# Five matmuls in place of six for units 2 and 14 of batches 1 to 7, with their sum and difference on VectorE

## The chip, the cores and the metric

The kernel runs on one core of a Trainium2 chip. The metric is the device time of one execution in microseconds (us). The engines are called by the profile's names: PE is TensorE, DVE is VectorE, ACT is ScalarE, POOL is GpSimd, SP is SyncE, which here issues DMAs. "L444" is line 444 of the kernel before.

## What is computed

The input x has 8 batches of 3072 rows with 256 columns. Each batch goes through a Fourier transform along both axes, of which the real part is kept; then each row goes through a layer with three weight matrices, an elementwise maximum of the three products, and an output matrix:

```python
X = np.fft.fft(np.fft.fft(x, axis=1), axis=2).real      # 8 x 3072 x 256
X = X.reshape(24576, 256)
h = np.maximum(np.maximum(X @ w1, X @ w2), X @ w3)      # 24576 x 768
out = h @ w_out                                         # 24576 x 256
```

## The kernel before, in words

The transform along the rows of a batch ends in two tables for half of its rows, an even part tE and an odd part tO (128 x 1536 in bf16); a row and its mirror row are the sum and the difference of the two. The transform along the columns is folded into the weights: gE, gO and gD hold (w2 - w1) and (w3 - w1) behind it, index 0 for the first difference and 1 for the second, with gD = -2 gO but for a correction of one row. With them the hidden layer is max(0, second product, third product), and what w1 gives is added in the last step.

**Units.** The main loop runs over 8 batches x 18 units. A unit is one of three blocks of 512 row pairs and one of six slices of 128 hidden columns (UNITS = 18, NJC = 6). The unit with number g gives two tiles of 128 x 512, hp for the rows and hm for their mirror rows. `begin(g, ...)` makes hp, `finish(g, ...)` makes hm, usually one unit later.

- A unit that is not split has six matmuls of 512 columns. `unit_plus` puts gE and gO products of both differences into two PSUM banks, pse2 and pse3 (L436, L437). `unit_out` makes hp: ACT writes relu(pse2) as stmp (L450), DVE takes the maximum with pse3 (L451). `unit_minus` then adds the gD products to the same two banks (L444), which turns the sum into the difference, and `unit_out` makes hm from them.
- A split unit (odd numbers from 7 on) has five. `third(g)` runs two units ahead (one ahead for unit 7): two matmuls give the even product e3 (L755) and the odd product d3 (L757) of the second difference in two banks; ACT copies -0.5 x d3 to SBUF as odd3 (L759); DVE adds a term to e3 and writes even3 (L760); POOL makes even3 + odd3 and even3 - odd3, plus3 and minus3 (L764). `begin` has the two matmuls of the first difference alone (L771, L772) and one DVE operation that takes the maximum with 0 and plus3 (L773); `finish` has one gD matmul and the like with minus3 (L785).

**Banks.** PSUM has eight banks here: ps_f with three, used by `third` and by all pieces of the transform and of the output step that need one; ps_l1 with two for pse2; ps_w3 with one for pse3 of even units; ps_o with two for the output step's po and for pse3 of odd units.

**Order.** The schedule is written out by hand: each engine runs its instructions in the order of the program. For each g the loop does this: if the unit before is split, `finish` of it, then `begin(g)`; else `begin(g)` first and then `finish` of the unit before. Then `third` of a coming unit; `scatter`, which issues waiting indirect stores on POOL; ten steps of the output step of an earlier block (`l2_some(10)`: matmuls L460, L475 and L483 into po, then DVE's ot at L488 and the stores on SP); and last what a plan has put at this place, pieces of the next batch's transform above all. The pieces that matter here are s (L369: two matmuls into a bank of ps_f, emptied by ACT at L372) after units 1, 2 and others, and k (L411: some six small matmuls into a bank of ps_f, emptied by ACT at L413) after units 12 to 16. `x0` (L399) waits for a small POOL copy (`u`, L394). Batch 7 has no pieces of a next batch.

Of the kernel before, what the change touches and what calls it, by code (L numbers as in the profile page):

```python
# [9 lines left out]
FP32 = mybir.dt.float32  # L10
BF16 = mybir.dt.bfloat16
INT32 = mybir.dt.int32
AX = mybir.ActivationFunctionType
ALU = mybir.AluOpType
# [36 lines left out]
def kernel(  # L51
# [9 lines left out]
    nc = tc.nc  # L61

    B, S, D = x.shape
# [3 lines left out]
    TOKB = 512  # L67
    NHALF = 1536
    UNITS = 3 * NJC
# [9 lines left out]
    ps_f = ctx.enter_context(tc.tile_pool(name="ps_f", bufs=3, space=bass.MemoryType.PSUM))  # L79
# [94 lines left out]
    for r in (0, 6, 11):  # L174
        n = {0: 6, 6: 5, 11: 4}[r]
# [25 lines left out]
    def scal(out, in0, s1, op0, s2=None, op1=None, eng=None):  # L201
# [8 lines left out]
                                   op0=ALU.mult, op1=ALU.add)  # L210
# [3 lines left out]
                                   op0=ALU.mult, op1=ALU.add)  # L214
# [5 lines left out]
                                   op0=ALU.mult, op1=ALU.add)  # L220
# [7 lines left out]
    half = gen.tile([128, 256], FP32, tag="half")  # L228
# [7 lines left out]
    for fc in range(2):  # L236
        scal(pf[:, fc:fc + 1], pidx, float(128 * fc), ALU.add)
        nc.vector.scalar_tensor_tensor(
            out=vm[:, fc * 256:(fc + 1) * 256].rearrange("p (k c) -> p k c", c=128),
            in0=dvec.unsqueeze(1).to_broadcast([128, 2, 128]), scalar=pf[:, fc:fc + 1],  # L240
            in1=half.rearrange("p (k c) -> p k c", c=128), op0=ALU.mult, op1=ALU.add)
# [12 lines left out]
                          in_=par.unsqueeze(1).to_broadcast([128, 2, 2]))  # L254
# [311 lines left out]
    def scatter():  # L566

        while waiting:
            at_row, lo, ot = waiting.pop(0)
            stored(nc.gpsimd.indirect_dma_start(  # L570
                out, bass.IndirectOffsetOnAxis(
                    ap=rows_m[0:128 - lo, at_row: at_row + 1], axis=0),
                ot[lo:128, 256:512], None), "scattered", ("scattered", "direct"))
            nc.gpsimd.memset(mark, 0.0)

    def l2_some(n):
        while n > 0 and l2_queue:
            try:
                next(l2_queue[0])
                n -= 1  # L580
            except StopIteration:
                l2_queue.pop(0)
# [37 lines left out]
    for (s0, s1) in HALVES:  # L620
        for h in range(2):
            load_x(1, s0, s1, h)
        if s0 == 0:
            nc.gpsimd.dma_start(out=wout_bf.rearrange("p (jc c) -> p jc c", jc=NJC),
                                in_=moe_w_out.rearrange("(jc p) c -> p jc c", jc=NJC))
# [15 lines left out]
    for u in range(3):  # L641
# [7 lines left out]
                       in1=adj.unsqueeze(1).to_broadcast([128, B, 12]), op=ALU.add)  # L649
# [4 lines left out]
    ps_w3 = ctx.enter_context(tc.tile_pool(name="ps_w3", bufs=1, space=bass.MemoryType.PSUM))  # L654
# [3 lines left out]
    s_pool = ctx.enter_context(tc.tile_pool(name="sums", bufs=3))  # L658
# [79 lines left out]

    sums = {}

    def is_split(g):
        return g % 2 == 1 and 7 <= g < B * UNITS

    def operands(g):
        b, u = divmod(g, UNITS)
        blk, jc = divmod(u, NJC)
        mm = mixes[b]
        ts = slice(blk * TOKB, (blk + 1) * TOKB)
        return slice(jc * 128, (jc + 1) * 128), mm.tE[:, ts], mm.tO[:, ts], mm.vb[:, ts], jc

    def third(g):

        js, te, to, vb, jc = operands(g)
        e3 = ps_f.tile([128, TOKB], FP32, name="e3", tag="ps")
        nc.tensor.matmul(e3, gE[1][:, js], te, start=True, stop=True)  # L755
        d3 = ps_f.tile([128, TOKB], FP32, name="d3", tag="ps")
        nc.tensor.matmul(d3, gD[1][:, js], to, start=True, stop=True)  # L757
        even3, odd3 = (s_pool.tile([128, TOKB], FP32, name=n, tag=n) for n in ("even3", "odd3"))
        nc.scalar.activation(out=odd3, in_=d3, func=AX.Copy, scale=-0.5)  # L759
        nc.vector.scalar_tensor_tensor(out=even3, in0=vb, scalar=wcol[:, jc:jc + 1], in1=e3,  # L760
                                       op0=ALU.mult, op1=ALU.add)
        sums[g] = [s_pool.tile([128, TOKB], BF16, name=n, tag=n) for n in ("plus3", "minus3")]
        for dst, op in zip(sums[g], (ALU.add, ALU.subtract)):
            nc.gpsimd.tensor_tensor(out=dst, in0=even3, in1=odd3, op=op)  # L764

    def begin(g, dst):

        js, te, to, _, jc = operands(g)
        if is_split(g):
            pse2 = ps_l1.tile([128, TOKB], FP32, name="pse2", tag="pse2")  # L770
            nc.tensor.matmul(pse2, gE[0][:, js], te, start=True, stop=False)  # L771
            nc.tensor.matmul(pse2, gO[0][:, js], to, start=False, stop=True)  # L772
            nc.vector.scalar_tensor_tensor(out=dst, in0=pse2, scalar=0.0, in1=sums[g][0],  # L773
                                           op0=ALU.max, op1=ALU.max)
            return (pse2,)
        pses = unit_plus(te, to, jc, TOKB, *((ps_o, "po") if g % 2 else (ps_w3, "pse3")))
        unit_out(pses, dst, TOKB)
        return pses

    def finish(g, pses, dst):  # L780

        js, te, to, _, jc = operands(g)
        unit_minus(pses, to, jc)
        if is_split(g):
            nc.vector.scalar_tensor_tensor(out=dst, in0=pses[0], scalar=0.0, in1=sums.pop(g)[1],  # L785
                                           op0=ALU.max, op1=ALU.max)
        else:
            unit_out(pses, dst, TOKB)

    prev = None  # L790
    for g in range(B * UNITS):
        b, u = divmod(g, UNITS)
        blk, jc = divmod(u, NJC)
        mm = mixes[b]
        last = b == B - 1 and blk == 2
        if jc == 0:
            hp = h_pool.tile([128, NJC, TOKB], BF16, name="hp", tag="hp")
            hm = h_pool.tile([128, NJC, TOKB], BF16, name="hm", tag="hm")
            if last:
                flipped = []  # L800
                for t, name in ((mm.tE, "tEr"), (mm.tO, "tOr")):
                    fl = h_pool.tile([128, TOKB], BF16, name=name, tag=name)
                    flipped.append(fl)
                    nc.gpsimd.tensor_copy(fl, t[:, 3 * TOKB - 1: 2 * TOKB - 1: -1])
        if prev is not None and is_split(prev[0]):
            finish(*prev)
            prev = None
        pses = begin(g, hp[:, jc, :])
        if prev is not None:
            finish(*prev)  # L810
        prev = (g, pses, hm[:, jc, ::-1] if last else hm[:, jc, :])
        for lead in (1, 2):
            if is_split(g + lead) and (lead == 1) == (g + lead == 7):
                third(g + lead)
        scatter()
        l2_some(10)
        if b == B - 1 and u in (1, 3):
            if u == 1:
                middle = l2_mid()
            next(middle, None)  # L820
        for fn in plan.get((b, u), ()):
            fn()
        if jc == NJC - 1:
            l2_some(1000)
            if g == B * UNITS - 1:
                finish(*prev)
            l2_queue.append(l2_last(hp, hm, mm.tE, mm.tO, flipped) if last else
                            l2_block(b, blk, hp, hm, mm.tE, mm.tO))
# [32 lines left out]
```

## Time and profile before

| | |
|---|---|
| three runs | 406.56, 406.56, 405.85 us; median 406.56 us |
| the profiled execution | 405.21 us, of which the span of its instructions is 403.4 us |
| granted clock of PE, mean over the span | 0.991 |
| pace | 45.5 us a batch |

The pace is the distance of equal instructions in neighbouring batches: the matmul L755 of unit 3 starts at 169.63 us in batch 3 and at 215.09 us in batch 4. A profile names each engine's busy time, the span in 40 equal slices, whom an engine waited for, and every instruction's start and length. The costliest groups of the units, one line each (line, engine, operation, result and operands with their shapes, count; busy us, mean ns of one; idle us of the engine before them and what ended it):

```profile
L450 ACT ACTIVATE stmp<-pse 128x512 bf16<-128x512 f32 x150 | 89.9, 600 | 62.1 <-PE pse L444 45.2
L764 POOL TENSOR_TENSOR plus<-even,odd 128x512 bf16<-128x512 f32 x69 | 87.9, 1274 | 39.8 <-DVE even L760 32.2
L773 DVE SCALAR_TENSOR_TENSOR hp<-pse,plus 128x512 bf16<-128x512 f32 x69 | 47.6, 690 | 50.6 <-PE pse L772 21.1
L444 PE MATMUL pse<-tO,gD 128*128 128x512 bf16 x218 | 70.8, 379 | 1.0 <-DVE hp L451 0.4
L488 DVE TENSOR_TENSOR ot<-po,even 128x512 f32<-128x512 f32 x92 | 62.9, 683 | 0.0
L451 DVE TENSOR_TENSOR hp<-pse,stmp 128x512 bf16<-128x512 f32 x75 | 51.5, 686 | 10.3 <-ACT stmp L450 8.7
L760 DVE SCALAR_TENSOR_TENSOR even<-vb,wcol,e 128x512 f32<-128x512 bf16 x69 | 51.0, 739 | 0.0
L785 DVE SCALAR_TENSOR_TENSOR hm<-pse,minus 128x512 bf16<-128x512 f32 x69 | 47.2, 684 | 1.8 <-PE pse L444 0.4
L759 ACT ACTIVATE odd<-d 128x512 f32<-128x512 f32 x69 | 41.3, 598 | 6.6
```

The last column is read first: it says for which group its engine stood still. The mean of a matmul is its whole time through the array; matmuls follow each other more closely than that, so PE's pace is read from start to start in the timeline.

### The profile page before, as it was taken

Reading aid. Unit: us, or ns where it says so; the run is one execution under the profiler, and the core shown is the slowest. Engines: PE = TensorE matmul, PEld = TensorE weight load, DVE = VectorE, ACT = ScalarE, POOL = GpSimd, SP = SyncE. Lnnn points to the kernel's source line nnn. Section 1 sums busy time; section 2 is a strip of 40 time slices with the busy share of each in tenths; the row PEclk is TensorE's granted clock in tenths of the full one; section 3 lists DMA queues with packets and bytes.
Section 4 is the critical chain, followed back from the end, with each engine's and each line's share of the span. In section 5 each row is a group of like instructions: output and inputs, shape, how many; then the busy total and the mean of one; then the engine's idle time right before and its main releaser. Section 6 shows DMA issues by size and latency. Waiting matters only on the chain.

```text
span 403.4 us, 8304 instructions
## 1 busy us (share of the span) xinstructions
PE 383.7 (95%) x2695; PEld 236.7 (59%) x2743; DVE 319.6 (79%) x542; ACT 261.2 (65%) x466; POOL 322.1 (80%) x403
## 2 busy tenths in 40 slices
PE   7589899999999999999999999999999999999995
PEld 2245456656665566656665566656665566666574
DVE  7869887877887887877887887877887887887982
ACT  2565879768865778568875778568865546635430
POOL 7376279787988799897988799897988699788991
PEclk9799999999999999999999999999999999999999
DMA  8999968495765958394764958495532653322225
GB/s 122 196 187 174 176 180 158 118 169 131 178 141 121 185 147 166 109 178 116 192 149 109 190 146 160 115 160 143 149 107 78 149 141 100 94 70 67 89 81 142
DMA packets 69692, 56.30 MB, mean 140 GB/s; under 512 B 35040, under 2 KB 65248, under 8 KB 68452
## 3 DMA queue, kind: packets, MB, share of 16 engines
q0 software_dynamic: 23376, 26.27, 34.5%
q1 hardware_dynamic: 45106, 28.86, 27.6%
q10 hardware_dynamic: 1168, 0.65, 0.6%
q8 instruction: 21, 0.34, 0.3%
q14 instruction: 21, 0.17, 0.2%
HBM read 38.15 MB, written 31.71 MB: 173 GB/s over the span
## 4 chain that ended last, share of the span: by engine, by line
PE 73%; DMA 9%; DVE 5%; issue 5%; POOL 4%; ACT 3%; SPq 1%; ACTq 0%; DVEq 0%; POOLq 0%
PE po L460 25%; PE pse L444 10%; PE pse L436 7%; DMA out_dram<-ot 6%; PE pse L437 5%; PE pse L771 4%; PE po L483 4%; PE d L757 3%; PE pse L772 3%; PE e L755 3%; DVE even L760 3%; PE ps L411 2%; DMA xt<-in_x_dram 2%; PE pl L475 2%; POOL minus L764 2%
## 5 line engine op out<-in xcount | busy, mean ns | idle before, releaser
L450 ACT ACTIVATE stmp<-pse 128x512 bf16<-128x512 f32 x150 | 89.9, 600 | 62.1 <-PE pse L444 45.2
L764 POOL TENSOR_TENSOR plus<-even,odd 128x512 bf16<-128x512 f32 x69 | 87.9, 1274 | 39.8 <-DVE even L760 32.2
L570 POOL DMA_INDIRECT out_dram<-ot,rows_m x92 | 102.4, 1113 | 17.9 <-issue 8.3
L773 DVE SCALAR_TENSOR_TENSOR hp<-pse,plus 128x512 bf16<-128x512 f32 x69 | 47.6, 690 | 50.6 <-PE pse L772 21.1
L764 POOL TENSOR_TENSOR minus<-even,odd 128x512 bf16<-128x512 f32 x69 | 87.6, 1269 | 0.0
L460 PE MATMUL po<-wout_bf,hp 128*128 128x256 bf16 x576 | 86.1, 273 | 0.3
L460 PE MATMUL po<-wout_bf,hm 128*128 128x256 bf16 x576 | 78.6, 273 | 0.0
L444 PE MATMUL pse<-tO,gD 128*128 128x512 bf16 x218 | 70.8, 379 | 1.0 <-DVE hp L451 0.4
L460 PEld LDWEIGHTS <-hp 128*128 128x128 bf16 x576 | 56.4, 98 | 26.1
L460 PEld LDWEIGHTS <-hm 128*128 128x128 bf16 x576 | 56.4, 98 | 16.3
L488 DVE TENSOR_TENSOR ot<-po,even 128x512 f32<-128x512 f32 x92 | 62.9, 683 | 0.0
L451 DVE TENSOR_TENSOR hp<-pse,stmp 128x512 bf16<-128x512 f32 x75 | 51.5, 686 | 10.3 <-ACT stmp L450 8.7
L436 PE MATMUL pse<-tE,gE 128*128 128x512 bf16 x147 | 55.6, 378 | 1.6 <-ACT stmp L450 0.2
L451 DVE TENSOR_TENSOR hm<-pse,stmp 128x512 bf16<-128x512 f32 x75 | 51.7, 689 | 5.9 <-ACT stmp L450 2.1
L760 DVE SCALAR_TENSOR_TENSOR even<-vb,wcol,e 128x512 f32<-128x512 bf16 x69 | 51.0, 739 | 0.0
L437 PE MATMUL pse<-tO,gO 128*128 128x512 bf16 x130 | 49.2, 379 | 0.7 <-ACT tO L413 0.4
L785 DVE SCALAR_TENSOR_TENSOR hm<-pse,minus 128x512 bf16<-128x512 f32 x69 | 47.2, 684 | 1.8 <-PE pse L444 0.4
L759 ACT ACTIVATE odd<-d 128x512 f32<-128x512 f32 x69 | 41.3, 598 | 6.6
L129 ACT COPY xt<-xt 64x762 bf16<-64x762 bf16 (+1 forms) x48 | 40.2, 838 | 1.1
L372 ACT CAST tb<-ps 128x512 bf16<-128x512 f32 x46 | 24.8, 589 | 21.7 <-PE ps L369 21.7
L444 PEld LDWEIGHTS <-gD 128*128 128x128 bf16 x219 | 21.2, 97 | 23.2 <-issue 5.0
L483 PE MATMUL po<-gw,tO 128*128 128x512 bf16 x86 | 32.7, 380 | 0.0
(155 smaller groups left out, 462.4 us busy)
## 6 DMA issues: line engine op xcount, KB each, us to landing
yb<-db SPq DMA_DIRECT2D x7, 833.0 KB
xt<-in_x_dram POOLq DMA_DIRECT2D x14, 384.0 KB, 8.3
out_dram<-ot SPq DMA_DIRECT2D x56, 96.0 KB
out_dram<-ot SPq DMA_DIRECT2D x64, 64.0 KB
db<-tb SPq DMA_DIRECT2D x21, 192.0 KB
vb<-vd SPq DMA_DIRECT2D x23, 128.0 KB
xt<-in_x_dram POOLq DMA_DIRECT2D x7, 400.0 KB
xt<-in_x_dram POOLq DMA_DIRECT2D x7, 368.0 KB, 5.6
```

The lines of the kernel that those rows point to most:

```text
L436: nc.tensor.matmul(pse[:, 0:n], gE[i][:, js], te, start=True, stop=False)
L437: nc.tensor.matmul(pse[:, 0:n], gO[i][:, js], to, start=False, stop=True)
L444: nc.tensor.matmul(pse, gD[i][:, js], to, start=False, stop=True, skip_group_check=True)
L450: nc.scalar.activation(out=stmp[:, 0:n], in_=pses[0][:, 0:n], func=AX.Relu)
L451: nc.vector.tensor_tensor(out=dst, in0=src3, in1=stmp[:, 0:n], op=ALU.max)
L460: nc.tensor.matmul(po, hcols(jc), wout_bf[:, jc * 256:(jc + 1) * 256], start=False, stop=(jc == NJC - 1), skip_group_check=True)
L483: nc.tensor.matmul(po, to[:, cp], gw[:, 256:768], start=True, stop=True)
L488: nc.vector.tensor_tensor(out=ot.rearrange("p (h c) -> p h c", h=2), in0=po.rearrange("p (h c) -> p h c", h=2), in1=lin.unsqueeze(1).to_br ...
L570: stored(nc.gpsimd.indirect_dma_start(out, bass.IndirectOffsetOnAxis(ap=rows_m[0:128 - lo, at_row: at_row + 1], axis=0), ot[lo:128, 256:51 ...
L760: nc.vector.scalar_tensor_tensor(out=even3, in0=vb, scalar=wcol[:, jc:jc + 1], in1=e3, op0=ALU.mult, op1=ALU.add)
L764: nc.gpsimd.tensor_tensor(out=dst, in0=even3, in1=odd3, op=op)
L773: nc.vector.scalar_tensor_tensor(out=dst, in0=pse2, scalar=0.0, in1=sums[g][0], op0=ALU.max, op1=ALU.max)
```

## The change

Units 2 and 14 of batches 1 to 7 (14 units), which were not split, are split too, in a form of their own. Their `third` runs one unit ahead, before the `third` of the odd unit behind them. Their e3 goes into the bank of ps_w3 and d3 into one of ps_f. ACT makes no odd3 and POOL no sums: DVE makes plus3 and minus3 straight from d3's bank and even3, with the factors -0.5 and 0.5.

```diff
+    def on_dve(g):
+        return g >= UNITS and g % UNITS in (2, 14) and g < B * UNITS
+
     def is_split(g):
-        return g % 2 == 1 and 7 <= g < B * UNITS
+        return (g % 2 == 1 and 7 <= g < B * UNITS) or on_dve(g)
...
     def third(g):
 
         js, te, to, vb, jc = operands(g)
-        e3 = ps_f.tile([128, TOKB], FP32, name="e3", tag="ps")
+        pool3, tag3 = (ps_w3, "pse3") if on_dve(g) else (ps_f, "ps")
+        e3 = pool3.tile([128, TOKB], FP32, name="e3", tag=tag3)
         nc.tensor.matmul(e3, gE[1][:, js], te, start=True, stop=True)
         d3 = ps_f.tile([128, TOKB], FP32, name="d3", tag="ps")
         nc.tensor.matmul(d3, gD[1][:, js], to, start=True, stop=True)
-        even3, odd3 = (s_pool.tile([128, TOKB], FP32, name=n, tag=n) for n in ("even3", "odd3"))
-        nc.scalar.activation(out=odd3, in_=d3, func=AX.Copy, scale=-0.5)
+        even3 = s_pool.tile([128, TOKB], FP32, name="even3", tag="even3")
+        if not on_dve(g):
+            odd3 = s_pool.tile([128, TOKB], FP32, name="odd3", tag="odd3")
+            nc.scalar.activation(out=odd3, in_=d3, func=AX.Copy, scale=-0.5)
         nc.vector.scalar_tensor_tensor(out=even3, in0=vb, scalar=wcol[:, jc:jc + 1], in1=e3,
                                        op0=ALU.mult, op1=ALU.add)
         sums[g] = [s_pool.tile([128, TOKB], BF16, name=n, tag=n) for n in ("plus3", "minus3")]
+        if on_dve(g):
+            for dst, half in zip(sums[g], (-0.5, 0.5)):
+                nc.vector.scalar_tensor_tensor(out=dst, in0=d3, scalar=half, in1=even3,
+                                               op0=ALU.mult, op1=ALU.add)
+            return
         for dst, op in zip(sums[g], (ALU.add, ALU.subtract)):
             nc.gpsimd.tensor_tensor(out=dst, in0=even3, in1=odd3, op=op)
...
         for lead in (1, 2):
-            if is_split(g + lead) and (lead == 1) == (g + lead == 7):
+            if is_split(g + lead) and (lead == 1) == (g + lead == 7 or on_dve(g + lead)):
                 third(g + lead)
```

The order around unit 2 (unit 14 is alike, with 12, 13, 14 and 15), as the two programs have it:

| loop turn | before | after |
|---|---|---|
| 1 | begin 1, finish 0, third 3, l2, pieces | begin 1, finish 0, **third 2**, third 3, l2, pieces |
| 2 | finish 1, begin 2 (four matmuls), l2, pieces | finish 1, begin 2 (two matmuls), l2, pieces |
| 3 | begin 3, finish 2 (two matmuls), third 5, l2, pieces | finish 2 (one matmul), begin 3, third 5, l2, pieces |

## The prediction

> **What bounds the kernel now.** I read the page from the top (busy shares, the 40 slices), then the waits of TensorE (PE) alone from 60 to 400 us, then the timeline at the places that the change touches, then the groups by shape for the prices. The busy shares and two of the slice rows:
>
> ```profile
> PE 383.7 (95%) x2695; PEld 236.7 (59%) x2743; DVE 319.6 (79%) x542; ACT 261.2 (65%) x466; POOL 322.1 (80%) x403
> ...
> PE   7589899999999999999999999999999999999995
> DVE  7869887877887887877887887877887887887982
> ```
>
> PE is at 9 tenths from the sixth slice to the last but one; no other engine is. The waits of PE from 60 to 400 us, the whole answer:
>
> ```profile
> PE psx L399 <- POOL x0u L394: 1.2, 6, 0.2
> ```
>
> In 340 us PE waited 1.2 us for anybody. So there is no slack on it: a matmul taken from PE shortens the run by its step, and any new wait of PE lengthens the run by its length. The timeline of batch 4 around the place where unit 2's work will stand (columns: start, duration, engine, line, operation, result and operands):
>
> ```profile
> 214.23 0.38 PE L771 MATMUL pse<-tE,gE 128*128 128x512 bf16 x1
> 214.44 0.38 PE L772 MATMUL pse<-tO,gO 128*128 128x512 bf16 x1
> 214.66 0.59 PE L444 MATMUL pse<-tO,gD 128*128 128x512 bf16 x2
> 214.93 0.69 DVE L773 SCALAR_TENSOR_TENSOR hp<-pse,plus 128x512 bf16<-128x512 f32 x1 [0.64 <-PE pse L772]
> 215.08 0.60 ACT L450 ACTIVATE stmp<-pse 128x512 bf16<-128x512 f32 x1 [0.93 <-PE pse L444]
> 215.09 0.38 PE L755 MATMUL e<-tE,gE 128*128 128x512 bf16 x1
> ...
> 215.31 0.38 PE L757 MATMUL d<-tO,gD 128*128 128x512 bf16 x1
> 215.52 0.82 PE L460 MATMUL po<-wout_bf,hm 128*128 128x256 bf16 x6
> 215.71 0.69 DVE L451 TENSOR_TENSOR hm<-pse,stmp 128x512 bf16<-128x512 f32 x1
> ...
> 216.18 0.38 PE L483 MATMUL po<-gw,tO 128*128 128x512 bf16 x1
> ...
> 216.31 0.74 DVE L760 SCALAR_TENSOR_TENSOR even<-vb,wcol,e 128x512 f32<-128x512 bf16 x1
> 216.39 0.38 PE L460 MATMUL po<-wout_bf,hp 128*128 128x256 bf16 x2
> ...
> 216.71 0.62 PE L369 MATMUL ps<-xt,tab 128*64 128x512 bf16 x4
> ```
>
> Matmuls overlap, so I count steps from start to start: 0.215 us for 512 columns (214.23, 214.44, 214.66), 0.11 us for 256 (six from 215.52 to 216.18). VectorE (DVE) starts one 0.69 us operation 0.60 us after the other (215.71, 216.31). It starts 0.11 us after the matmul that it waits for (L772 ends at 214.82, L773 starts at 214.93), and a matmul that waits for DVE starts 0.05 to 0.06 us after it (a hp ending at 38.07 releases the L444 matmul at 38.12). One DVE operation that reads the result of the one before starts 0.03 us behind its end (L22 and L24, 8.69 and 0.43 long, then 9.15).
>
> **The change, part by part.** It touches 14 units, two in each of seven batches.
>
> *Matmuls.* Each unit had six (L436/L437 four, L444 two) and gets five (two new ones for e3 and d3, two for its begin, one for its finish). PE's built list is 28 rows shorter, 14 matmuls and their 14 weight loads. 14 x 0.215 = **-3.0 us**.
>
> *The bank of e3.* This is the step that decides. e3 of unit 2 (14) takes the one bank of ps_w3, and its matmul is issued one unit ahead, directly behind the two L444 matmuls of unit 0 (12). These write that same bank, and its last reader is unit 0's hm operation on DVE (L451), which itself needs ScalarE's L450 of the other bank. In the built program of the changed kernel this matmul waits for that hm operation. Before, the next tenant was unit 2's own begin, a whole unit later, and it found the bank free. In the rows above, the place is where L755 now starts, at 215.09; the hm ends at 215.71 + 0.69 = 216.40, and e3 can start at 216.46. PE stands for 216.46 - 215.09 = 1.37 us; it works in order, so everything behind waits too, the L460 matmuls first. I read the same two rows at all 14 places (where the matmul's record is missing, its weight load's end plus 0.115 us, as at the places that have both). Unit 2: 1.37 us in six batches, 1.54 in batch 2. Unit 14: 1.66 us in batches 1 to 5, where ScalarE first empties a tO bank (L413) and L450 comes 0.3 us later, and 1.37 in batches 6 and 7. Sum: 6 x 1.37 + 1.54 + 5 x 1.66 + 2 x 1.37 = **+20.8 us**.
>
> *The sums on DVE.* The unit loses two L451 operations (0.69) and gets even3 (row L760, 0.74), two sums and two of the begin/finish form (L773 0.69, L785 0.68): +2.1 us a unit, some 30 us in all, so DVE would be busy about 349 us of some 427. The two sums, one PSUM and one fp32 SBUF operand and a bf16 result, have no row: L488 (PSUM and fp32, 0.68) and L760 (0.74) bound them; I take 0.69, by L773, which has its operation and its result type. Most of this lies beside PE, in DVE's 84 us of idle time. Two places are not covered.
>
> First, the bank of d3 is now free only when the second sum has read it, where ScalarE's copy (L759) freed it before; of the pieces that follow in the same unit, the second takes this bank in the built program. Unit 2 of batch 4: e3 at 216.46, even3 216.95 to 217.69, sums 217.72 to 218.41 and 218.32 to 219.01. PE after e3 has three steps more (d3 and unit 3's pair), so the l2 matmuls begin at 217.32, the first s piece at 218.51 (1.19 later, as 215.52 to 216.71 above) and the second at 218.78; it may start at 219.07: 0.29 us. Unit 14 in the same way: e3 at 247.31, second sum done at 249.86, second k piece due at 249.51, free at 249.92: 0.41 us.
>
> Second, unit 14's hp operation stands on DVE behind even3 of unit 15, an ot (L488) and hm of unit 13. That chain ends at 252.31; the finish matmul is due at 252.11 and starts at 252.37: 0.26 us. For unit 2 the same chain ends at 221.45 and the matmul is due at 221.73: nothing.
>
> Batch 7 has no pieces behind it. So 6 x 0.29 + 6 x (0.41 + 0.26) = **+5.7 us**, bounded by nothing (if ScalarE and DVE, which catch up during the wait, take it up) and by twice as much (if another ot falls into each chain).
>
> *Work that goes elsewhere.* ScalarE loses two L450 a unit (14 x 1.2 = 17 us) and GpSimd gets nothing; neither is what PE waits for, so I cost it at nothing. The cover is PE's own queue; were it gone, the most to gain would be the 1.2 us of psx waits. GpSimd's sums for units 3 and 15 come some 2.6 us later, behind two more operations of DVE, while PE is 1.7 us later; their readers have a unit's length in hand. Transfers keep their order, so I cost them at nothing as well.
>
> *Sum.* -3.0 + 20.8 + 5.7 = **+23.5 us**. The profiled execution took 405.2 us (span 403.4 and 1.8 around it), which gives 428.7; the runs' median is 1.4 us above it, and on 406.56 the sum gives 430.1. I predict 430.
>
> **The clock.** A wait of this length may also cost granted clock. The windows of the trace show half clock once:
>
> ```profile
> 10.00:12.00 2.00, 0.52 (x3) 0.13 (x2) 1.68 (x4) 0.23 (x1) 1.99 (x4) 1.00 1.26 201
> 12.00:14.00 2.00, 0.84 (x6) 0.25 (x5) 1.36 (x6) 1.13 (x3) 1.63 (x5) 1.00 1.31 195
> 14.00:16.00 2.00, 1.01 (x5) 0.42 (x5) 1.65 (x12) 1.18 (x3) 0.26 (x1) 0.54 1.27 210
> 16.00:18.00 2.00, 0.91 (x3) 0.38 (x4) 1.90 (x5) 1.21 (x3) 0.00 (x0) 0.50 1.14 247
> ...
> 22.00:24.00 2.00, 1.28 (x11) 0.66 (x9) 1.20 (x2) 1.97 (x5) 1.96 (x3) 1.00 0.73 225
> 24.00:26.00 2.00, 1.32 (x11) 0.68 (x12) 0.01 (x1) 1.04 (x4) 2.00 (x4) 1.00 1.21 179
> ```
>
> The second column is the window's length, then PE's busy time; the clock is the third from the end. It fell after 4 us in which PE worked 1.36 us, and held at 1.00 where it worked 2.60 of 4 (22 to 26 us). A single new wait leaves PE more than half of any 4 us, so I keep the full clock. The Trainium skill (TensorE: Matmul & The Clock Gate, section "A second HAM failure mode: psum-queue depth-cycling") speaks against me: at bf16 and 512 columns, short idles between groups that cycle through PSUM banks made the clock swing between half and full. That page of the skill (section "What's actually happening") puts the fall after an idle window of about 3.4 us, which the trace's 4 us agree with and a wait of 1.7 us would not reach.
>
> **Rivals.**
> - *Faster: the bank is free in time.* If hm of unit 0 (12) were done less than 0.215 us after e3 is due, the saved matmul would win: with no wait -3.0 us, 403.5. The place is the bank of ps_w3, the price 0.215 us a unit. All 14 places show 1.37 us or more, and what sets it, L450 then L451, is unchanged. 4%.
> - *Slower still: DVE falls behind.* Around the changed units DVE has 4.9 us of work in one unit, where PE needs 2.6. If its queue is not worked off before the next unit's banks are wanted, each of the 12 units with pieces loses one more DVE step of 0.6 us: +7.2, 437. Against it: the unit after has only two or three DVE operations. 12%.
> - *The clock halves behind each wait.* The half-clock stretch above cost 0.46 x 2 + 0.50 x 4 + 0.24 x 2 = 3.4 us (the 20 to 22 window has 0.76); 14 of them are +48, 478. 3%.
> - *The change does not do what it says.* The built list has the matmuls gone and the sums on DVE: under 1%.
>
> **How the numbers follow.** Forecast 80%, the others as above. The low end leaves out the 5.7 us of second waits (424.4) and lets PE win back some 3 us of them elsewhere: 421. The high end is the DVE rival with 1 us: 438. Faster than before by over 0.2% (0.8 us, about what a measurement of this kernel can tell from no change) 4%, within it 1%, slower 95%.
>
> **What would show it.** Right: the e3 matmul of the 14 units with an idle time before it, put down to DVE hm L451, of 1.2 to 1.5 us each (the idle column counts from the end of the matmul before, 0.16 us later than its step); shorter ones at the second s or k piece, put down to the second sum; PE's share falling to about 90%; the clock at 1.00. Wrong: no idle time before these matmuls; idle time before others in larger sum; DVE at 9 tenths throughout; a clock under 1.00 in the later slices.

## The result, and the profile after

| | before | after |
|---|---|---|
| median of six runs, us | 406.04 (405.48 to 406.56) | 431.0 (430.25 to 431.74) |
| ratio | | 1.061 (95% interval 1.060 to 1.063) |
| span of the profiled execution, us | 403.4 | 429.5 |
| distance of two batches, us | 45.5 | 48.9 |

The kernel became 6% slower, 25 us, where 23.5 were forecast. The profiled execution is the slowest of the six runs, so its span stands 26.1 us above that of before, and sums are made against the median here. The busy shares and the slices:

```profile
PE 385.1 (90%) x2681; PEld 236.4 (55%) x2729; DVE 346.6 (81%) x584; ACT 247.5 (58%) x438; POOL 322.1 (75%) x403
...
PE   6588899899898998899898998899798998899885
...
DVE  6969788877888888887887888887788888887892
```

PE has 14 matmuls less and yet a longer span; its nines are broken by an eight (once a seven) every two or three slices. VectorE gained 27 us of work and stands at 7 or 8 tenths nearly everywhere; its nines are the second, the fourth and the last slice but one. The waits of PE from 60 us to the end, the whole answer (us in total, times, longest):

```profile
PE e L759 <- DVE hm L451: 18.8, 14, 2.1
PE pse L444 <- DVE hp L784: 1.9, 2, 1.2
PE ps L411 <- DVE minus L771: 1.6, 6, 0.3
PE ps L369 <- DVE minus L771: 1.0, 6, 0.2
```

Where before there was one row of 1.2 us there are four, and all of them name VectorE. 14 waits are at the new e3 matmul, one for each changed unit. The timeline at unit 2 of batch 4, the place that the prediction worked through:

```profile
225.95 0.59 PE L444 MATMUL pse<-tO,gD 128*128 128x512 bf16 x2
...
226.37 0.60 ACT L450 ACTIVATE stmp<-pse 128x512 bf16<-128x512 f32 x1 [0.93 <-PE pse L444]
...
227.00 0.69 DVE L451 TENSOR_TENSOR hm<-pse,stmp 128x512 bf16<-128x512 f32 x1
...
227.74 0.38 PE L759 MATMUL e<-tE,gE 128*128 128x512 bf16 x1 [1.19 <-DVE hm L451]
...
229.00 0.69 DVE L771 SCALAR_TENSOR_TENSOR plus<-d,even 128x512 bf16<-128x512 f32 x1
...
229.61 0.68 DVE L771 SCALAR_TENSOR_TENSOR minus<-d,even 128x512 bf16<-128x512 f32 x1
...
230.34 0.41 PE L369 MATMUL ps<-xt,tab 128*64 128x512 bf16 x2 [0.16 <-DVE minus L771]
```

The two L444 matmuls start at 225.95, so the next was due 2 x 0.215 us later, at 226.38; it starts at 227.74, 0.05 us after hm ends at 227.69. That is 1.36 us (the idle column shows 1.19, since it counts from the end of the matmul before). The last row is the second s piece, held by the second sum. The granted clock was 1.00 here, and in every window of 50 us from 50 to 400 us (the window's length, busy time of PE, PEld, VectorE, ScalarE and GpSimd, then the clock):

```profile
200.00:250.00 50.00, 46.42 (x327) 28.74 (x331) 40.79 (x64) 32.33 (x57) 40.63 (x49) 1.00 0.67 142
```

### The profile page after: what moved, and what is told of

It is laid out like the page before. It is cut to its first block, busy times and chain, and to the rows that moved or that the text cites. A ratio compares the mean times of both kernels' runs of the same rounds, so it can differ in the third digit from the quotient of the medians.

```text
span 429.5 us, 8247 instructions
## 1 busy us (share of the span) xinstructions
PE 385.1 (90%) x2681; PEld 236.4 (55%) x2729; DVE 346.6 (81%) x584; ACT 247.5 (58%) x438; POOL 322.1 (75%) x403
## 4 chain that ended last, share of the span: by engine, by line
PE 62%; DVE 14%; POOL 8%; issue 6%; ACT 5%; DMA 4%; DVEq 0%; ACTq 0%; POOLq 0%
PE po L460 21%; PE pse L444 8%; PE pse L436 6%; DVE even L766 4%; PE pse L437 4%; PE e L759 4%; PE pse L782 3%; PE po L483 3%; PE pse L783 3%; DVE hm L451 3%; POOL minus L775 3%; PE d L761 2%; DVE minus L771 2%; ACT stmp L450 2%; POOL plus L775 2%
## 5 line engine op out<-in xcount | busy, mean ns | idle before, releaser
L450 ACT ACTIVATE stmp<-pse 128x512 bf16<-128x512 f32 x122 | 72.9, 598 | 57.8 <-PE pse L444 41.6
L784 DVE SCALAR_TENSOR_TENSOR hp<-pse,plus 128x512 bf16<-128x512 f32 x83 | 57.1, 687 | 33.6 <-PE pse L783 18.3
L444 PE MATMUL pse<-tO,gD 128*128 128x512 bf16 x203 | 67.4, 379 | 3.9 <-DVE hp L784 1.9
L460 PEld LDWEIGHTS <-hp 128*128 128x128 bf16 x576 | 56.4, 98 | 26.1
L766 DVE SCALAR_TENSOR_TENSOR even<-vb,wcol,e 128x512 f32<-128x512 bf16 x83 | 61.4, 740 | 6.5 <-PE e L759 6.5
L796 DVE SCALAR_TENSOR_TENSOR hm<-pse,minus 128x512 bf16<-128x512 f32 x83 | 56.9, 686 | 10.8 <-PE pse L444 10.8
L451 DVE TENSOR_TENSOR hp<-pse,stmp 128x512 bf16<-128x512 f32 x61 | 41.9, 687 | 9.4 <-ACT stmp L450 8.7
L759 PE MATMUL e<-tE,gE 128*128 128x512 bf16 x83 | 31.4, 378 | 19.3 <-DVE hm L451 18.8
L451 DVE TENSOR_TENSOR hm<-pse,stmp 128x512 bf16<-128x512 f32 x61 | 42.0, 689 | 5.5 <-ACT stmp L450 2.7
L436 PE MATMUL pse<-tE,gE 128*128 128x512 bf16 x119 | 45.0, 378 | 1.5 <-ACT stmp L450 0.2
L437 PE MATMUL pse<-tO,gO 128*128 128x512 bf16 x103 | 39.0, 379 | 0.7 <-ACT tO L413 0.4
```

The source lines that it names most:

```text
L436: nc.tensor.matmul(pse[:, 0:n], gE[i][:, js], te, start=True, stop=False)
L437: nc.tensor.matmul(pse[:, 0:n], gO[i][:, js], to, start=False, stop=True)
L444: nc.tensor.matmul(pse, gD[i][:, js], to, start=False, stop=True, skip_group_check=True)
L450: nc.scalar.activation(out=stmp[:, 0:n], in_=pses[0][:, 0:n], func=AX.Relu)
L451: nc.vector.tensor_tensor(out=dst, in0=src3, in1=stmp[:, 0:n], op=ALU.max)
L460: nc.tensor.matmul(po, hcols(jc), wout_bf[:, jc * 256:(jc + 1) * 256], start=False, stop=(jc == NJC - 1), skip_group_check=True)
```

## The experiments

Three theories were set against each other. The *queue theory* is the prediction's: PE, which works in order, stands until operations on VectorE have been reached and done, and pays each such wait in full. The *shared-bank theory* says that the single bank of ps_w3 is the cause, and that e3 elsewhere would cost nothing. The *load theory* says that VectorE's extra operations cost the time, wherever they stand. Ratios are to the kernel before, run on the same chip (95% intervals in brackets); times are medians.

**early_bank: the wait without the change.** The kernel before, and in it (cut: the two helpers, and the part of `begin` that then makes the other bank's two matmuls alone):

```diff
+        if early(g + 1):           # units 2 and 14 of batches 1 to 7
+            pse3_early(g + 1)      # the two gE/gO matmuls into ps_w3's bank
         for lead in (1, 2):
             if is_split(g + lead) and (lead == 1) == (g + lead == 7):
                 third(g + lead)
```

> The kernel before, with all its six matmuls and its sums; only the two matmuls of units 2 and 14 (batches 1 to 7) into the bank of ps_w3 are issued one unit ahead, directly behind the finish of unit 0 (12). Queue theory (PE stands until the hm operation of unit 0 or 12 has read the bank): the 14 first waits alone, 406.0 + 20.8 = 427, each 1.2 or 1.5 us of idle time before the early matmul. Load theory (DVE's extra operations cost the time, wherever they stand): no extra operation, so 406.

Measured: 427.2 us, ratio 1.052 (1.046 to 1.059). The waits of PE:

```profile
PE pse L752 <- DVE hm L451: 18.9, 14, 2.2
PE psx L399 <- POOL x0u L394: 1.2, 6, 0.2
```

No operation was added to any engine, and 21 to 22 of the 25 us are there. The load theory does not hold for the main part: it is the place of one accumulation (two matmuls) in PE's order. A small part is the clock: at the end of the longest of the waits (2.17 us, up to 210.22) it fell to half, and stayed there for 3.4 us (columns as above).

```profile
206.00:210.00 4.00, 2.06 (x17) 1.21 (x16) 2.22 (x4) 3.19 (x6) 3.83 (x5) 1.00 0.51 139
210.00:213.40 3.40, 2.95 (x10) 1.57 (x11) 0.92 (x2) 1.01 (x2) 1.84 (x4) 0.50 0.96 137
```

The profiled run and one more of the four, with a mean clock of 0.987, took 427.9 and 427.8 us; the other two, with 0.991, took 426.1 and 426.6.

**bank_psf: e3 in another pool.**

```diff
-        pool3, tag3 = (ps_w3, "pse3") if on_dve(g) else (ps_f, "ps")
+        pool3, tag3 = ps_f, "ps"
```

> The changed kernel with e3 of the 14 units in a bank of ps_f, as the odd units have it; place and sums unchanged. Shared-bank theory (the single bank of ps_w3 is the whole cause): the first waits go, 404 to 411. Queue theory: ps_f has three banks for four tiles, and the fourth, d3 of unit 3 (15), waits for even3 of unit 2 (14), which stands on DVE behind the same hm operation: 1.36 and 1.67 us again, now before d3 and put down to even3, with the later waits nearly gone: 425. Load theory: 431.

Measured: 424.1 us, ratio 1.046 (1.039 to 1.053).

```profile
PE d L761 <- DVE even L766: 18.5, 14, 1.5
PE pse L444 <- DVE hp L784: 0.8, 2, 0.6
PE e L759 <- ACT tO L413: 0.5, 1, 0.5
```

The shared-bank theory falls. With e3 in another pool the 14 waits are still there, as long as before; they stand three matmuls later, at d3 of unit 3 (15), and name even3 instead of hm. even3 of unit 2 is behind hm of unit 0 in VectorE's order, so neither bank comes free before that hm is done. The later waits nearly vanish, since the sums start earlier against PE: in batch 4 the first sum starts 0.05 us behind d3 of unit 3 (225.12 and 225.07), in the changed kernel 0.62 us (229.00 and 228.38). That is most of the 6 to 7 us that this kernel gains on the changed one.

**behind_l2: the same work later in the turn.**

```diff
         l2_some(10)
+        if on_dve(g + 1):
+            third(g + 1)
```

(and not ahead of it)

> The changed kernel with the two early matmuls and the DVE operations of units 2 and 14 issued behind the ten l2 steps of the same turn; bank and sums unchanged. Shared-bank theory: the hm operation is then done when e3 is due, no wait is left, 403 to 404. Queue theory: the wait at e3 goes (0 to 0.15 us), but the sums now stand later on DVE and the hp operation behind them holds up the finish matmul, 0.8 us in units 2, 1.4 to 1.6 in units 14, about 1.9 in batch 7: 406.0 - 3.0 + 18.6 = 422. Load theory: 431.

Measured: 421.9 us, ratio 1.040 (1.032 to 1.048). The whole answer for the waits of PE:

```profile
PE pse L444 <- DVE hp L784: 17.5, 14, 2.0
```

The wait at e3 has gone and another has come up at the finish of the same unit: 0.80 us of idle time in four units 2 of seven, 1.47 or 1.48 in five units 14 of seven, and 1.5 and 2.0 in batch 7. A matmul that can be had in time is of no use when what hangs on it on VectorE comes too late for the next one.

**sums_pool: the sums on GpSimd, as the odd units have them.**

```diff
-        if not on_dve(g):
+        if True:
...
-        if on_dve(g):
+        if False:
             for dst, half in zip(sums[g], (-0.5, 0.5)):
```

> The changed kernel, with the sums of the 14 units made as in the odd units (ScalarE copies d3, GpSimd adds and subtracts); e3 keeps its bank and its place. Queue theory: first waits stay (+20.8), the matmuls stay saved (-3.0), the waits behind the sums on DVE go: 424, up to 428 if GpSimd's longer queue delays the psx matmul. Load theory: DVE has 10 us more than before in place of 27, so a third of the loss or so: 413 to 416.

Measured: 429.3 us, ratio 1.058 (1.052 to 1.064).

```profile
PE e L759 <- DVE hm L451: 18.3, 14, 1.6
PE psx L399 <- POOL x0u L394: 5.8, 5, 1.2
PE pse L444 <- DVE hp L784: 0.6, 1, 0.6
```

The load theory wanted a third of the loss; nearly all of it is left. The waits behind VectorE's sums are gone, as the queue theory has it, but the psx matmul waits 0.9 to 1.2 us in five batches, behind two sums more in GpSimd's queue. Those were priced at up to 4 us and came to 4.6 more than the 1.2 us of before.

**lead2_dve: two units ahead.** On top of bank_psf:

```diff
-            if is_split(g + lead) and (lead == 1) == (g + lead == 7 or on_dve(g + lead)):
+            if is_split(g + lead) and (lead == 1) == (g + lead == 7):
```

> The changed kernel with the early work of units 2 and 14 issued two units ahead, as the odd units have it, and e3 in a bank of ps_f; the sums stay on DVE. Queue theory: the two matmuls now stand ahead of the output step's first matmuls with their banks free, even3 stands on DVE ahead of the hm operation instead of behind it, and the hp operation of unit 2 is done at 219.9 where the finish matmul is due at 220.1 (times of batch 4 before), so that little waiting is left: -3.0 to +3, 402.5 to 408.5. Load theory: DVE has its extra 27 us as in the changed kernel, so 425 to 431.

Measured: 409.1 us, ratio 1.008 (1.005 to 1.010).

```profile
PE pse L444 <- DVE hp L784: 2.9, 4, 1.2
PE psx L399 <- ACT tb L376: 0.9, 3, 0.3
PE ps L411 <- ACT even L479: 0.9, 1, 0.9
PE psx L399 <- POOL x0u L394: 0.6, 2, 0.4
```

This decides against the load theory: VectorE is busy for 342 us here against 347 in the changed kernel, with the same number of operations, and 22 of the 25 us are gone. It came out 0.6 us above the range of the queue theory. What is left is mostly at the finish of units 14 (0.12 us of idle time in four batches, 0.48 and 0.33 in the fifth and sixth) and of the two units of batch 7 (1.0 and 1.2 us), 3.4 us in all. With the 0.9 us before the L411 matmul, the 0.3 us that the psx matmul waits more than before, and up to 0.165 us for each of these nine new waits, which the idle column leaves out, that makes some 6 us. Less the 3.0 us of saved matmuls, 3 us are left, against 3.4 measured.

**lead2_pool: the same with GpSimd's sums.** lead2_dve with the edit of sums_pool.

> As the run with the lead of two units, but the sums of the 14 units made by ScalarE and GpSimd. Queue theory: no wait of PE for DVE; GpSimd has 34 us more in units around the x0 piece, and in the run with its sums one unit ahead the psx matmul waited 1.2 us in each of six batches, so 403 plus up to 7: 404 to 411. Load theory: DVE has 10 us more, 410 to 416.

Measured: 431.6 us (427.7 to 436.3), ratio 1.064 (1.060 to 1.069). The queue theory's range ends 21 us below this, the load theory's 16.

```profile
PE psx L399 <- POOL x0u L394: 13.7, 6, 2.6
PE pse L444 <- DVE hp L784: 5.9, 9, 1.4
PE ps L411 <- ACT odd L765: 1.1, 2, 0.6
```

My sum was wrong in treating the psx wait of sums_pool as a length of its own (it also counted six such waits; sums_pool has five). It is the difference between PE's arrival and GpSimd's: with the wait of 1.37 us at e3 taken away, PE reaches psx that much earlier, and 1.2 us becomes 2.6. Most batches take 48.9 us, as in sums_pool (49.1): GpSimd's queue up to that copy sets them, and whatever PE wins before it is given back there. The timeline of GpSimd ahead of the copy in batch 4:

```profile
236.38 1.26 POOL L775 TENSOR_TENSOR plus<-even,odd 128x512 bf16<-128x512 f32 x1
237.61 1.26 POOL L775 TENSOR_TENSOR minus<-even,odd 128x512 bf16<-128x512 f32 x1
238.81 0.26 POOL L394 COPY x0u<-xt 128x49 bf16<-128x49 bf16 x1
```

The copy stands right behind the sums of the odd unit, without a gap. Between the copy of batch 2, at 139.94 us, and that of batch 3, at 188.81, GpSimd stood still for more than 0.31 us once: 1.85 us, for even3, behind the first copy. The waits at L444 hang on GpSimd too, at least in part: the hp that PE waits for there is made from plus3, and VectorE waited for that 17 times.

```profile
DVE hp L784 <- POOL plus L775: 18.9, 17, 1.8
```

The clock adds to the loss. Behind two of the four psx waits of 2.6 us, in batches 3 and 5, it was granted at half for 3.4 us; the row of the first:

```profile
189.80:193.20 3.40, 3.40 (x15) 1.86 (x13) 2.04 (x3) 2.02 (x3) 1.44 (x3) 0.50 0.85 234
```

The six runs, in order of time, have mean clocks of 0.983, 0.979, 0.976, 0.975, 0.974 and 0.972: the spread from 427.7 to 436.3 us goes with the clock. How much of it the clock costs was not tried. The four shortest, up to 432.2, have a median of 430.4, so the loss does not hang on the two longest.

**lead2_u2: only where nothing waits.** lead2_dve with

```diff
-        return g >= UNITS and g % UNITS in (2, 14) and g < B * UNITS
+        return g >= UNITS and g % UNITS == 2 and g < (B - 1) * UNITS
```

> The run with a lead of two units, e3 in ps_f and the sums on DVE, for unit 2 of batches 1 to 6 alone. In that run no finish of a unit 2 with pieces behind it waited for its hp operation regularly, those of units 14 waited 0.29 us and those of batch 7 about 1 us. Queue theory: six matmuls less and no new wait, -6 x 0.215 = -1.3 us, about 404.5, ratio 0.997. Load theory: DVE has 13 us more, so part of a loss remains, above 407.

Measured: 405.0 us, ratio 0.999 (0.997 to 1.001). The loss is gone, and VectorE's added work in six units costs nothing that can be measured. The forecast gain of 1.3 us (0.3%) would lie at the lower end of the interval, which holds 1 as well: it is neither shown nor refuted. PE waits as little as before:

```profile
PE psx L399 <- ACT tb L376: 0.9, 3, 0.3
PE psx L399 <- POOL x0u L394: 0.2, 1, 0.2
PE pse L444 <- DVE hp L784: 0.2, 1, 0.2
```

**not_last: batch 7 as before.**

```diff
-        return g >= UNITS and g % UNITS in (2, 14) and g < B * UNITS
+        return g >= UNITS and g % UNITS in (2, 14) and g < (B - 1) * UNITS
```

> The changed kernel with the change left out of batch 7 alone (12 units in place of 14). Queue theory: the two units of batch 7 cost 1.37 + 0.88 - 0.22 and 1.37 + 1.37 - 0.22 us, the second terms being the waits of their finish matmuls, so 4.6 us less: 426.4. If batch 7 cost what the prediction gave it (1.37 - 0.22 each): 428.7.

Measured: 426.3 us, ratio 1.050 (1.047 to 1.054). 4.7 us less than the changed kernel (some 4.5 by the ratios), for two units of 14: the last batch costs about twice what the prediction gave it, and the two L444 waits are gone:

```profile
PE e L759 <- DVE hm L451: 16.2, 12, 1.9
PE ps L411 <- DVE minus L771: 1.6, 6, 0.3
PE ps L369 <- DVE minus L771: 0.9, 6, 0.2
```

## Why the prediction was right, step by step

- **Matmuls saved, -3.0 us.** Right: PE has 14 instructions less, and matmuls follow each other at the same steps as before. No run shows this gain by itself: lead2_u2, with six of them, cannot tell 1.3 us from nothing.
- **The bank of e3, +20.8 us.** Right in place, cause and size. 18.8 us of idle time and 14 x 0.165 us between the end and the step of the matmul before are 21.1 us. Units 2 waited 1.36 us in every batch, units 14 1.66 us in batches 1 to 4 and 1.36 in 6 and 7. Batch 2 did not have its 1.54 us but 1.36: that value was read from one execution in which one operation happened to come late. One wait of the 14, unit 14 of batch 5, was 0.6 us longer than its like. What the prediction did not say, and bank_psf showed, is that the choice of the bank matters little: all that stands behind hm on VectorE is late by the same.
- **Later waits, +5.7 us.** Right for batches 1 to 6: 0.29 us at the second s piece (0.16 of idle time), 0.4 at the second k piece, 0.26 at the finish of units 14 (0.09). Wrong for batch 7, the one step that was mis-sized: "Batch 7 has no pieces behind it" was taken to mean no wait. The pieces would have been hit by the second sum, but they also cover VectorE's chain: without them the finish matmul is due earlier, and hp is not ready. It cost 0.88 and 1.37 us, 2.25 in all (not_last confirms it).
- **Work elsewhere, nothing.** Nearly: the psx matmul's waits fell to some 0.07 to 0.09 us of idle time from 0.2, a gain of under 1 us, within the most that was named.
- **The sum.** +23.5, with 2.3 for batch 7 and 0.6 for the one long wait, less 0.2 for batch 2 and some 0.8 at psx, gives 25.4; 25.0 were measured between the medians. The forecast time, 430, came nearer to the measured 431.0 than the sum did to 25.0, by luck: it started from 406.56 us, the median of three runs, 0.5 us above that of the six.
- **Rivals.** *Faster*: all 14 places waited, none below 1.3 us. *VectorE falls behind*: no row of PE's waits grows from unit to unit, and the next unit's hm follows on time. The clock did not halve behind each wait.
- **The clock.** It was 1.00 behind all 14 waits of the changed kernel. But the prediction's reason, that a single new wait leaves PE more than half of any 4 us, does not make this safe. In early_bank PE worked 2.06 of the 4 us before 210.0 and the clock fell to half; in the changed kernel, at its longest wait, PE worked 1.87 of the 4 us before 309.6 and it did not. Among four psx waits of 2.6 us in lead2_pool it fell behind two, though at each of the four PE worked 1.4 of the 4 us around the wait. What decides is not shown; the changed kernel's longest wait (2.13 us) was nearly as long as the one of early_bank, so that it kept its clock may have been luck. The Trainium skill's warning (TensorE: Matmul & The Clock Gate, "A second HAM failure mode: psum-queue depth-cycling") is not borne out in the changed kernel: 14 waits of up to 2.13 us of idle time between groups of 512-column matmuls, each for a PSUM bank, left the granted clock at 1.00. The Trainium skill puts the fall after an idle window of about 3.4 us (TensorE: Matmul & The Clock Gate, "What's actually happening"); taken as the length of a wait, as the prediction took it, this does not hold here, where it fell with waits of 2.2 and 2.6 us.

## What to carry to other kernels

Where one engine has no idle time, read a moved instruction at its new place: what is the last thing that must have happened there, and on whose queue does that stand. Count the price from the rows just ahead of that place, once for each time the loop passes it; it was seven times the matmuls saved here, and neither another bank nor a place a microsecond later took it away, only a place ahead of the operation that it waited behind (lead2_dve). The same place with the sums on GpSimd lost it all again (lead2_pool): a wait that is taken away can come back where another engine's queue sets the pace. And a piece of work that is hit by a wait is often the cover of another: where it is missing, price the place anew.

## What the runs showed of the hardware

- VectorE's operation with the factor, one PSUM and one fp32 SBUF operand and a bf16 result, 128 x 512, took 0.68 to 0.69 us, the same as with a bf16 operand. The first sum started 0.10 us behind the end of even3 (228.15 + 0.75, then 229.00), where 0.03 was taken from two operations in the start of the kernel.
- In three of the profiles one single wait of the row was longer than its like by 0.4 us or more (2.13 in place of 1.49 here, up to 2.2 in early_bank, 1.9 in not_last). At the one in the changed kernel ScalarE's L450 started at 308.16, 1.0 us behind the end of the matmul that it follows (306.81 + 0.38), with a tO bank and a copy of x ahead of it. Why that copy stood later than in other batches is open.
- A wait of little more than 2 us can cost granted clock. It was at half for 3.4 us from the end of a wait of 2.17 us (early_bank) and from 0.7 us behind two waits of 2.56 and 2.57 us (lead2_pool), and stayed at 1.00 behind waits of 2.13 us (the changed kernel) and 2.58 and 2.59 us (lead2_pool). With PE busy throughout, such a stretch costs 1.7 us, an estimate from these rows (half of 3.4).
